# A decode step with gated attention: gate weights and w_down with w_q's second part exchange buffers, and 128 columns of w_o come by a DMA of their own

## The chip, the cores and the metric

The kernel runs on one core of one Trainium2 chip. Its time is the device time of one execution in microseconds (us), the median of some runs. All data is fp32. The engines named here: PE (TensorE, matrix products), DVE (VectorE), ACT (ScalarE), POOL (GpSimd), and SP (SyncE), which computes nothing and issues nearly all transfers. SBUF is the memory on the core with 128 partitions; PSUM takes what PE computes; HBM is the main memory.

## The reference

One decode step, for a batch of 2 and a width of 448. The input is normalised, goes through attention with 16 query heads over 8 cached key/value heads of length 4096, and is gated by a small bilinear network:

```python
xn = layernorm(x)                                   # x: (2, 1, 448)
q = (xn @ wq)                                       # 16 heads of 256
p = softmax(q k^T * 256 ** -0.5)                    # k_cache, v_cache: (2, 8, 4096, 256)
s = (p v) @ wo                                      # wo: (4096, 448)
h = (xn @ w_gate) * (xn @ w_up)                     # 448 -> 1792
g = silu(h @ w_down)
return x + s * g
```

The two caches alone hold 134 MB, the weights 24 MB more. Every byte of them is used once.

## The kernel before

**Recording.** The kernel doesn't call the engines itself. `Recorder` (L206) notes each operation with what it reads and writes; `settle` (L88) derives from it which operation must wait for which; `issue` of `Flow` (L144) then writes each engine's instructions in the recorded order. So each engine runs its own list in order, and an instruction that waits holds back all behind it on that engine. Since every operation passes through the recorder, nearly all rows of the profile have the one line L220; they are told apart by tile names. `loop` (L112) turns PE's part of the seven equal turns into a loop; the other engines' lists are written out.

**Memory.** Two ring buffers of 64 KB a partition (`ring`, L242) and one slot of 52.5 KB a partition (`slot`, L243) take all large loads. Eight PSUM banks, two pairs (`s`) and four alone (`o`, `cb`, `sm`, `wide`), take the products.

**Loads.** `plan` (L275) notes the loads, `issue(n)` (L263) records the next n of them on SP, so the order in which SP issues them is the order of the plan:

- w_q's first part (`wq0`) into ring buffer 1, its first 7,168 columns
- gate and up weights (`wg wu`, the tensor wgu) into the slot
- w_down and w_q's second part (`wd wq1`, the tensor wdq) into ring buffer 0
- the keys of the first item (`k0`, the tensor named first) into ring buffer 1, behind `wq0`
- then for i = 0 to 13 the values of item i with the keys of item i + 1 (`vk`), 8 MB each, into ring buffers 0, 1, 0, 1 and so on; after the second of them w_o's first 24 blocks of 448 columns (`wo`), into the slot
- at the end keys and values of the last items, and the last 8 blocks of w_o (`wo2`), in seven pieces (the tensors last0 and last1)

`issue(4)` (L291) records the first four at the very start; none of them waits. The first turn records two vk loads and then w_o's; each later turn records two. A load that goes into a buffer waits on SP until the last reader of what lies there is done.

**Compute.** An item is one key/value head of one batch row; there are 16. Before the loop, the normalisation runs on DVE and POOL, PE computes the query's first half (`query(0)`, reading `wq0`), the gate (`ffn_in`, reading `wg` and `wu`; `ffn_out`, reading `wd`), the query's second half (`query(1)`, reading `wq1`), and the first scores (`scores(0)`, reading `k0`), in this order (L517 to L523). Each of the seven turns (L524) does two items. For item i: softmax of its scores (DVE, PE, ACT), the product with the values on PE (`values`), a copy of the result on DVE, a copy of the next item's query into one of two small tiles (`qc`, L537, on ACT), and the next item's scores on PE, which read that copy. At a turn's end the two items are combined and divided by their sums. After the loop come the last two items, interleaved with the product with w_o (`project`, L506, over 24 blocks; `project_last`, L512, over the last 8), and the gate; one store of 56 KB ends the kernel.

**Host side.** Inputs are laid out for the loads before the launch (L584 to L622): each load is one array of 128 rows, and a row goes to one partition.

Of the kernel before, what the change touches and what calls it, by code (L numbers as in the profile page):

```python
# [8 lines left out]
B, D = 2, 448  # L9
# [11 lines left out]
LATE = 24  # L21
PART = 14 * (D + 512)
EPS = 1e-5
WQ = 14 * 512
LEAD = 0


class Flow:
# [115 lines left out]
    def issue(self):  # L144
        nc = self.nc
        lead = nc.alloc_semaphore("lead")
        for _ in range(LEAD):
            nc.vector.sem_inc(lead)
# [72 lines left out]
        return add  # L221


def gated_decode_block(nc, x, first, vk, last0, last1, wq0, wdq, wo, wgu, out):
    flow = Flow(nc)
    PE, DVE, ACT, POOL, SP = [getattr(flow, e) for e in ("PE", "DVE", "ACT", "POOL", "SP")]
    names = iter(range(1000))
# [14 lines left out]
    ring = Ring("ring", [128, 2 * ROW], 2, 512)  # L242
    slot = Ring("slot", [128, PART], 1, 512)  # L243
# [7 lines left out]
    def two():  # L251
        pairs.append(pairs.pop(0))
        return pairs[-1]

    def bank(name=None):
        return banks[name] if name else two()[:, 0]
# [6 lines left out]
    def issue(n=1):  # L263
        for names, place, src, cuts in todo[:n]:
            t = place()
            width = ROW if not names[0].startswith("w") else src.shape[1] // len(names)
            for i, name in enumerate(names):
                loaded[name] = t[:, i * width:(i + 1) * width]
            if names == ["wd", "wq1"]:
                loaded["wd"], loaded["wq1"] = t[:, :14 * D], t[:, 14 * D:]  # L270
            for lo, hi in zip(cuts, cuts[1:]):
                SP.dma_start(t[:, lo:hi], src[:, lo:hi])
        del todo[:n]

    def plan(names, place, src, cuts=None):  # L275
        todo.append((names.split(), place, src, cuts or [0, src.shape[1]]))
# [2 lines left out]
        return ring.bufs[1][:, WQ:]  # L279

    plan("wq0", lambda: ring.bufs[1], wq0)
    plan("wg wu", slot, wgu)
    plan("wd wq1", lambda: ring.bufs[0], wdq)
    plan("k0", behind, first)
    for i in range(LAST):
        plan(f"v{i} k{i + 1}", ring, vk[i])
# [2 lines left out]
    plan(f"k{LAST + 1} v{LAST}", ring, last0, [0, ROW, 2 * ROW])  # L289
    plan(f"v{LAST + 1} wo2", ring, last1, [0, 6144, ROW, *(ROW + i * D for i in (5, 7, 8))])  # L290
    issue(4)  # L291


# [131 lines left out]
    def query_of(i):  # L425
        g, b = divmod(i, B)
        return qT[g // 4][:, b, g % 4].rearrange("p d r j -> p d (r j)")

    def scores(i, q, s, halves=(0, 1)):
        k = loaded[f"k{i}"].rearrange("p (h d c n) -> p h d c n", h=2, d=2, c=NT)  # L430
        for h in halves:
            for d in range(2):
                for c in range(NT):
                    PE.matmul(s[W * c:W * (c + 1), h, :], q[:, d], k[:, h, d, c, :], start=d == 0, stop=d == 1)
        return s
# [31 lines left out]
    def softmax(i, s):  # L467
        m = peak(s)
        return turned(exponential(i, s, m, peak_of_all(m)), work["pT"]())
# [4 lines left out]
    def total(add):  # L474
        sm = bank("sm")
        PE.matmul(sm[:, :B], add.rearrange("p a r j -> p (a r j)"), su, start=True, stop=True)
        DVE.reciprocal(over, sm[:, :B])

    def values(i, pT, o):

        for e in range(KB):
            h, t, at = e // 8, e % NT, e % 8 * 2 * W
            PE.matmul(o[W * t:W * (t + 1), :], pT[:, h, at:at + 2 * W:2],
                             loaded[f"v{i}"][:, e * 512:(e + 1) * 512], start=e < NT, stop=e >= KB - NT)

    def combine(ob):
        cb = bank("cb")
        src = ob.rearrange("p s (e d c k) -> p s e d c k", e=2, d=2, c=NT)
        for e in range(2):
            for c in range(NT):  # L490
                PE.matmul(cb[W * c:W * (c + 1), :B * 64], add_blocks[:, e].rearrange("p r j -> p (r j)"),
                                 src[:, :, e, :, c, :], start=e == 0, stop=e == 1)
        return cb[:, :B * 64]

    def turn(oT, g, cb):
        DVE.transpose(oT[:, g].rearrange("p d r (b j) -> p b d r j", b=B),
                      cb.rearrange("p (b d r j) -> p b d r j", b=B, d=2, r=REP))
# [26 lines left out]
    for first in range(0, LAST, B):  # L524
        flow.turn = first
        issue(2)
        if first == 0:
            flow.turn = None
            issue()
            flow.turn = first  # L530
        for i in range(first, first + B):
            p = softmax(i, s)
            o = bank("o")
            values(i, p, o)
            DVE.tensor_copy(ob[:, i % B], o)
            q = copy()
            ACT.copy(q, query_of(i + 1))  # L537
            s = scores(i + 1, q, two())
        total(add_head)
        cb = combine(ob)  # L540
        t = work["h"]()[:, :B * 64]
        DVE.tensor_tensor(t.rearrange("p (s k) -> p s k", s=B), cb.rearrange("p (s k) -> p s k", s=B),
                          over[:, :, None].to_broadcast([128, B, 64]), op=OP.mult)
        turn(oT, first // B, t)
# [19 lines left out]
    t = work["h"]()  # L564
# [62 lines left out]
```

## Time and profile before

| | |
|---|---|
| time, median of 3 runs | 378.86 us (378.81 to 379.39) |
| the profiled execution: its own time | 379.15 us |
| its span, first to last instruction | 377.8 us |
| PE / DVE / ACT / POOL busy, share of the span | 50% / 20% / 8% / 1% |
| data read from HBM | 158.54 MB, 420 GB/s over the span |

A transfer passes over up to 16 DMA engines at once. A packet in the rows of transfers is one piece that one of them moves. "DMA share" in the rows of a stretch is the mean share of the 16 engines' time that the packets started in this stretch take, so a short stretch can show over 1. "us to landing" is from SP's issue to the last byte. Matmuls are written as inner x columns, then the output's shape. An entry in square brackets tells how long the engine stood idle ahead of a row and what ended it. The median of three runs and the profiled execution differ by 0.29 us.

### The profile page before, as it was taken

To read this page: it belongs to the slowest core of one execution; us is meant where nothing else is said; L and a number is where in the kernel's file an instruction comes from. 1 tells how busy PE (TensorE), PEld (TensorE's weight loads), DVE (VectorE), ACT (ScalarE), POOL (GpSimd) and SP (SyncE) were. 2 spreads that over 40 slices of the span, in tenths; PEclk is the share of its full clock that TensorE was granted. 3 is DMA by queue.
4 is the path that set the end of the run, shared out by engine and by line. 5 is a ranking of instruction groups with operands and counts; after the bars stand their busy time and mean duration, and the time that the engine had idled before them with its cause. 6 is when DMAs were issued, how large, how long until landed. Compare 5 with 4: busy or idle time off the path is not lost. (4 is left out here: it accounts for less than half of the span.)

```text
span 377.8 us, 3298 instructions
## 1 busy us (share of the span) xinstructions
PE 189.9 (50%) x1474; PEld 57.6 (15%) x1474; DVE 75.5 (20%) x124; ACT 28.6 (8%) x58; POOL 2.4 (1%) x14
## 2 busy tenths in 40 slices
PE   0827391090730373727282719190909092808776
PEld 0201120020210020202020202020202020202223
DVE  2101013003040021312113211312130304030430
ACT  1101011001010001010101010101010101010120
POOL 0100000000000000000000000000000000000000
PEclk9968598577785585959687968776867766776999
DMA  8999979999999999899999999999999999989995
GB/s 340 474 437 410 412 281 430 402 397 437 433 476 444 444 430 423 382 438 444 444 437 444 444 437 444 430 409 395 444 444 444 437 444 444 437 389 406 435 421 233
DMA packets 3898, 158.68 MB, mean 420 GB/s; under 512 B 562, under 2 KB 692, under 8 KB 820
## 3 DMA queue, kind: packets, MB, share of 16 engines
q1 hardware_dynamic: 3888, 158.59, 97.5%
q8 instruction: 4, 0.07, 0.1%
q14 instruction: 2, 0.02, 0.0%
q10 hardware_dynamic: 4, 0.00, 0.0%
HBM read 158.54 MB, written 0.06 MB: 420 GB/s over the span
## 5 line engine op out<-in xcount | busy, mean ns | idle before, releaser
L220 PE MATMUL o<-ring,pT 128*32 128x512 f32 x480 | 82.4, 848 | 118.2 <-PEq L172 118.2
L220 PE MATMUL s<-ring,qc 128*32 128x512 f32 x448 | 50.7, 592 | 0.0
L220 PEld LDWEIGHTS o<-ring,pT 128*32 128x32 f32 x480 | 20.8, 149 | 167.2 <-issue 167.2
L220 DVE COPY ob<-o 128x512 f32<-128x512 f32 x14 | 9.7, 691 | 159.9 <-PE o L220 159.9
L220 ACT ACTIVATE p<-s,m 128x1024 f32<-128x1024 f32 x16 | 17.8, 1114 | 289.7 <-DVE m L220 289.7
L220 DVE TENSOR_REDUCE m<-s 128x1 f32<-128x1024 f32 x16 | 19.3, 1204 | 21.8 <-PE s L220 21.8
L220 DVE STREAM_TRANSPOSE pT<-p 128x1024 f32<-128x1024 f32 x15 | 18.7, 1245 | 19.1 <-ACT p L220 19.1
L220 PEld LDWEIGHTS s<-ring,qc 128*32 128x32 f32 x448 | 15.1, 110 | 33.2 <-issue 33.2
L220 PE MATMUL sm<-ident,m 128*1 128x128 f32 x16 | 4.4, 276 | 25.6 <-PEq L172 23.7
L220 DVE TENSOR_REDUCE mx<-sm 1x128 f32<-1x512 f32 x16 | 10.9, 679 | 8.1 <-PE sm L220 8.1
L220 PE MATMUL s<-slot,xnT 128*32 128x448 f32 x48 | 7.2, 748 | 7.4 <-DMA slot<-wgu 7.4
L220 PE MATMUL s<-ring,hT 128*32 128x448 f32 x28 | 5.5, 903 | 8.4 <-DMA ring<-wdq 8.4
L220 PE MATMUL sm<-one,mx 1*128 1x1 f32 x16 | 3.2, 201 | 12.9 <-PEq L172 12.1
L220 PE MATMUL s<-ring,xnT 128*32 128x512 f32 x48 | 8.1, 825 | 0.0
L220 PE MATMUL s<-ring,qT 128*32 128x512 f32 x64 | 7.5, 597 | 0.0
L220 PEld LDWEIGHTS sm<-ident,m 128*1 128x1 f32 x16 | 1.3, 79 | 35.1 <-issue 32.9
L220 DVE RECIPROCAL over<-sm 128x2 f32<-128x2 f32 x8 | 1.4, 171 | 23.9 <-PE sm L220 23.9
L220 PE MATMUL s<-ident,pT 2*128 2x2 f32 x4 | 0.6, 246 | 10.7 <-DVE pT L220 10.7
L220 PE MATMUL cb<-ob,add_blocks 128*32 128x128 f32 x128 | 5.2, 279 | 0.6 <-ACT ob L220 0.6
L220 PE MATMUL wide<-slot,oT 128*32 128x448 f32 x48 | 4.9, 539 | 0.0
L220 PEld LDWEIGHTS sm<-one,mx 1*128 1x128 f32 x16 | 2.3, 142 | 16.6 <-issue 15.7
L220 PE MATMUL s<-ring,slot 128*32 128x512 f32 x32 | 3.6, 596 | 1.1 <-DMA ring<-last 1.1
(65 smaller groups left out, 63.7 us busy)
## 6 DMA issues: line engine op xcount, KB each, us to landing
ring<-last SPq DMA_DIRECT2D x2, 4096.0 KB, 27.1
ring<-wdq SPq DMA_DIRECT2D x1, 6720.0 KB, 42.4
slot<-wgu SPq DMA_DIRECT2D x1, 6272.0 KB, 25.4
slot<-wo SPq DMA_DIRECT2D x1, 5376.0 KB, 51.1
ring<-first SPq DMA_DIRECT2D x1, 4096.0 KB, 51.4
ring<-wq SPq DMA_DIRECT2D x1, 3584.0 KB, 11.0
ring<-last SPq DMA_DIRECT2D x1, 3072.0 KB, 21.9
ring<-last SPq DMA_DIRECT2D x1, 1120.0 KB, 24.4
```

What stands on the lines that cost most here:

```text
L220: self.flow.record(self.engine, lambda: method(out, *args, **kw), writes, reads, name == "dma_start")
```

## The change

Four things change.

1. The loads of gate and up weights and of w_down with w_q's second part exchange their places: the former goes into ring buffer 0, the latter into the slot. The order of the loads stays.
2. w_o's first load is 128 columns narrower. These 128 columns come by a second DMA right behind it into the same place; its source is an array of 4 groups of 33 rows of 128 columns, of which 32 rows each are read (the 33rd row is filler and isn't read).
3. The copy of the next item's query runs on POOL, not on ACT.
4. `LEAD` is 48: DVE's list begins with 48 instructions that each add one to a semaphore that nobody waits for.

```diff
-LEAD = 0
+LEAD = 48
+SHARE = 4
+COLS = 128
...
-def gated_decode_block(nc, x, first, vk, last0, last1, wq0, wdq, wo, wgu, out):
+def gated_decode_block(nc, x, first, vk, last0, last1, wq0, wdq, wo, wox, wgu, out):
...
             width = ROW if not names[0].startswith("w") else src.shape[1] // len(names)
+            if names == ["wo"]:
+                width = LATE * D
...
             for lo, hi in zip(cuts, cuts[1:]):
                 SP.dma_start(t[:, lo:hi], src[:, lo:hi])
+            if names == ["wo"]:
+                SP.dma_start(t[:, cuts[-1]:LATE * D], wox[:, :128 // SHARE])
...
-    plan("wg wu", slot, wgu)
-    plan("wd wq1", lambda: ring.bufs[0], wdq)
+    plan("wg wu", lambda: ring.bufs[0], wgu)
+    plan("wd wq1", slot, wdq)
...
             q = copy()
-            ACT.copy(q, query_of(i + 1))
+            POOL.tensor_copy(q, query_of(i + 1))
...
-    wo, last[1] = c(wo[:, :LATE * D]), np.concatenate([last[1], wo[:, LATE * D:]], 1)
+    last[1] = np.concatenate([last[1], wo[:, LATE * D:]], 1)
+    wox = np.zeros((SHARE, 128 // SHARE + 1, COLS), np.float32)
+    wox[:, :-1] = wo[:, LATE * D - COLS:LATE * D].reshape(SHARE, 128 // SHARE, COLS)
+    wo = c(wo[:, :LATE * D - COLS])
```

More of the change, by code (lines that the diff above doesn't have):

```diff
@@ L619 @@
     nc = bacc.Bacc("TRN2", target_bir_lowering=False, num_devices=1, dynamic_dma_scratch_size=1024)
-    arrays = dict(x=x, first=first, vk=vk, last0=last[0], last1=last[1], wq0=wq0, wdq=wdq, wo=wo, wgu=wgu)
+    arrays = dict(x=x, first=first, vk=vk, last0=last[0], last1=last[1], wq0=wq0, wdq=wdq, wo=wo, wox=wox, wgu=wgu)
     args = [nc.dram_tensor(n, a.shape, mybir.dt.from_np(a.dtype), kind="ExternalInput").ap()
```

## The prediction

> **What bounds the kernel now.** I read the page first: span, slices, chain.
>
> ```profile
> span 377.8 us, 3298 instructions
> ...
> DMA  8999979999999999899999999999999999989995
> GB/s 340 474 437 410 412 281 430 402 397 437 433 476 444 444 430 423 382 438 444 444 437 444 444 437 444 430 409 395 444 444 444 437 444 444 437 389 406 435 421 233
> ...
> q8 instruction: 4, 0.07, 0.1%
> ...
> q10 hardware_dynamic: 4, 0.00, 0.0%
> HBM read 158.54 MB, written 0.06 MB: 420 GB/s over the span
> ...
> DMA 6%; PE 3%; ACT 0%; DVE 0%; issue 0%
> ```
>
> The DMA engines are at nine tenths nearly everywhere, and the bytes are fixed. Apart from the first and last slices, one slice falls clearly out of the row: the sixth (47 to 57 us), 281 GB/s. The chain shows only the end, because a transfer that merely queues isn't followed further back. So I next asked for stretches around the sixth slice (the columns that count here are the last two, DMA share and GB/s), and for a long stretch behind it.
>
> ```profile
> 1.70:51.50 49.80, 24.28 (x136) 6.20 (x140) 6.52 (x19) 4.51 (x9) 1.58 (x6) 0.79 1.00 425
> 51.50:53.50 2.00, 2.00 (x22) 0.61 (x16) 0.00 (x0) 0.94 (x1) 0.00 (x0) 1.00 0.04 16
> 53.50:55.30 1.80, 1.80 (x16) 0.39 (x18) 0.82 (x2) 0.00 (x0) 0.00 (x0) 1.00 0.00 0
> 115.00:340.00 225.00, 110.27 (x816) 33.55 (x816) 47.27 (x70) 14.72 (x33) 0.00 (x0) 0.73 1.00 432
> ```
>
> From 51.5 to 55.3 us the transfers stand still: 3.8 us. In the first 2 us 16 GB/s x 2.0 us = 32 KB still start, one row of k0 (4096 KB over 128 rows is 32 KB): fifteen engines are dry, one is behind. Elsewhere the rate is 432 GB/s at a share of 1.00. Who is late? SyncE's issues, then PE's work, tell it.
>
> ```profile
> 2.11 0.59 SPq L220 DMA_DIRECT2D ring<-first  x1
> 54.44 3.92 SPq L220 DMA_DIRECT2D ring<-vk  x2
> 58.40 0.44 SPq L220 DMA_DIRECT2D slot<-wo  x1
> 85.01 227.88 SPq L220 DMA_DIRECT2D ring<-vk  x12
> ```
> ```profile
> 34.74 0.97 PE L220 MATMUL s<-slot,oT 128*64 128x448 f32 x4
> 44.08 5.52 PE L220 MATMUL s<-ring,hT 128*32 128x448 f32 x28 [8.36 <-DMA ring<-wdq]
> 53.32 1.08 PE L220 MATMUL s<-ring,oT 128*64 128x512 f32 x4
> 54.33 3.64 PE L220 MATMUL s<-ring,qT 128*32 128x512 f32 x32
> ```
> ```profile
> ring<-first SPq DMA_DIRECT2D x1, 4096.0 KB, 51.4
> ring<-vk SPq DMA_DIRECT2D x1, 21.8
> ring<-vk SPq DMA_DIRECT2D x14, 29.3
> ```
>
> After k0 (the tile named first) SyncE has nothing it may issue until 54.44. The first vk transfer goes into ring buffer 0, where w_down and w_q's second part lie; their last reader is query(1), whose last matmuls start at 53.32 and end at 54.40. k0 has landed at 2.11 + 51.4 = 53.5, so the queue runs out first. This is the only place: the fourteen vk transfers take a median of 29.3 us from issue to landing, while 8,389 KB at 432 GB/s need 19.4; each waits some 10 us behind its predecessor.
>
> **The exchange of buffers.** Ring buffer 0 now holds the gate weights. Their last reader is the end of ffn_in, 34.74 + 0.97 = 35.7 us. SyncE's queue is in order and has only the four first issues ahead, so vk0 can be issued at 35.7, some 16 us before the queue would run dry. The order and sizes of the first four loads are the same, so wdq still releases PE at 44.08 and PE's work up to 58 us stays. vk1 needs ring buffer 1, free after scores(0) at 54.33 + 3.64 = 58.0 as before; by then vk0 is moving from 51.5 to about 71. w_o's load needs the slot free of query(1), 54.4, and is issued behind vk1 as before. vk2 was issued at 85.01 and is not needed before w_o's end near 109. No stall is late next: the whole stream behind k0 moves ahead, and releases move with landings, which keeps the 10 us.
>
> What it saves: 3.8 us of standing still, and a restart. The stretch to 51.5, the other start from empty, shows 425 against 432 GB/s: 49.8 x 7/432 = 0.8 us. For the restart I take that 0.8; bounds: 0.3 (a smaller dip), and 1.5, since vk0 landed at 54.44 + 21.8 = 76.2, 20.9 us after 55.3 instead of 19.4. **Minus 4.6 us** (minus 4.1 to 5.3).
>
> Against it: the hole also let the engine that lagged catch up. It ended k0 up to 2.0 us behind the others (53.5 against 51.5) and started vk0 with them. Without the hole its lag stays to the end. Why it lagged:
>
> ```profile
> q8 instruction: 1, 0.02, 6.0%
> ```
>
> That is the window from 82.5 to 83.5 us: an instruction fetch of 16 KB took 6.0% of 16 engine-microseconds, 0.96 us, on one engine. The page counts four of them, and the same is seen between 42.02 and 43.02 us, just ahead of the laggard. Do such lags reach the end now? Budget: start 1.7, 158.5 MB at 432 GB/s 366.9, hole 4.6: 373.2. The last piece lands at about 375.05 (below), so some 1.9 us are left, about one engine's lag. The end already pays one; a fifth laggard on another engine adds only what it lags more: 2.0 - 1.9, say **plus 0.1** (0 to 0.4). On the same engine as a later fetch it would add its whole lag (first rival).
>
> The Trainium skill, "Runtime: NRT & Kernel Launch", section "Instruction fetch mechanics", says that instructions are refilled in 16 KB blocks through a DMA queue of the sequencer's own, the cost "mostly hidden". The block agrees with the four packets (0.07 MB). Hidden holds for the waiting sequencer; where DMA is the bound, 0.96 us on one engine isn't hidden. By the rule the term would be 0 and the sum 0.1 lower.
>
> **The 128 columns.** w_o's load shrinks by 512 of 43,008 bytes a row, and 128 rows of 512 bytes come by a second DMA, whose source is led by 4. On how many engines does it run? Rows for one and for sixteen:
>
> ```profile
> p<-x ACTq DMA_DIRECT2D x2, 1.8 KB
> ```
> ```profile
> DMA packets 144, 0.06 MB, mean 96 GB/s; under 512 B 144, under 2 KB 144, under 8 KB 144
> ...
> q1 hardware_dynamic: 144, 0.06, 34.4%
> ```
>
> The two one-row loads of x made the four packets of q10: one of data and one of completion each, so one engine. The output's store (376.9 to 377.5 us) made 144: 128 rows and 16 completions. A source led by 4 lies between; I take four engines with 32 rows each. A row of 448 bytes cost at most 34.4% x 0.6 us x 16 / 128 = 0.026 us; the upper neighbour:
>
> ```profile
> ring<-last SPq DMA_DIRECT2D x1, 448.0 KB, 25.2
> ring<-last SPq DMA_DIRECT2D x1, 224.0 KB, 25.2
> ```
> ```profile
> 346.49 3.80 SPq L220 DMA_DIRECT2D ring<-last  x5
> ```
>
> These five issues end at 350.29; with 0.44 us for one (w_o's row) the last begins at 349.85 and lands at 375.05. The one ahead of it has equal latency, so its 224 KB (8 rows of 1,792 bytes an engine) took about 0.5 us, 0.06 a row. So four engines get 32 x 0.026 to 0.06 = 0.8 to 2.0 us; I take 0.8, nearer in size. What is left out, 8 x 512 bytes an engine at 27 GB/s (432/16), is 0.15 us off every engine. Where none of the four lags already, the end gains **0.15**; where one does, it loses 0.7 (to 1.85). Spread over all sixteen it is 8 rows, plus 0.05 to 0.35; on one engine, see the rivals. SyncE's extra issue, about 0.44 us like w_o's, lies in its wait from 58.8 to 85.
>
> The Trainium skill, "DMA: Bandwidth & Descriptors", "Rules for kernel authors", warns that a leading dimension below 16 confines a DMA to that many engines. It speaks against this edit, and makes four engines a rule rather than my choice. Here it costs nothing if those four have room; by the rule alone, without room, the sum would be 0.85 higher.
>
> **The copy of q, and 48 increments.**
>
> ```profile
> L220 ACT COPY qc<-qT 128x64 f32<-128x64 f32 x14 | 3.3, 233 | 0.0
> L220 POOL COPY add_blocks<-rows 128x64 f32<-128x64 f32 x1 | 0.2, 234 | 0.0
> L220 PE MATMUL s<-ring,qc 128*32 128x512 f32 x448 | 50.7, 592 | 0.0
> 7.26 0.61 DVE L220 TENSOR_REDUCE st<-p 2x1 f32<-2x448 f32 x1 [7.26 <-DMA p<-x]
> 9.11 0.07 DVE L220 DVE_READ_ACCUMULATOR pT<-p 2x1 f32 x1
> 26.59 4.71 PE L220 MATMUL s<-slot,xnT 128*32 128x448 f32 x24 [7.36 <-DMA slot<-wgu]
> ```
>
> Fourteen copies go from ACT to POOL: 0.233 against 0.234 us for the same shape. POOL has nothing else after 13 us; its copy waits for scores two steps back to leave the buffer, and only PE waits for it. The matmuls that read it have no idle time ahead of them (0.0), and values run before them. Cost 0; uncovered, 14 x 0.23 = 3.3 us of PE, itself behind transfers. The increments run on DVE ahead of its first work, which waits for x until 7.26 us. At most 0.07 us each (the smallest DVE row, an upper end) is 3.4 us; without x as cover that would still lie under PE's 7.36 us wait. Cost 0. They also make DVE's code 48 instructions longer, and the copies make ACT's 14 shorter, which can move a fetch in time; whose fetch is whose isn't shown. A fetch loads one engine by up to 0.96 us whenever it comes. Effect 0, bounds minus 0.96 and plus 0.96 (off or onto the worst laggard).
>
> **The tail** follows the last transfers.
>
> ```profile
> 346.49 21.88 DMA ring<-last
> ...
> 373.51 2.09 PE s L220 x64
> ```
>
> From 346.49 the chain is the queue; the last matmuls end at 373.51 + 2.09 = 375.6, half a microsecond behind the last landing, then two DVE operations and the store. All of this hangs on landings and shifts with them.
>
> **Sum.** -4.6 + 0.1 - 0.15 = -4.65; with the small bounds that point up I round to **-4.5 us**. The profiled execution took 379.15 (span 377.8), so 374.65; the median of the three runs is 0.29 lower, 378.86, so 374.4. I forecast 374.4, with 373.4 to 375.2 as this case's own range.
>
> **Rivals.** *Lags add up* (0.22): the laggard of 42 us, or one of the four engines with the 512-byte rows, is also one that a later fetch hits. Price 0.7 (rows) to 1.9 (fetch): 375.1 to 376.3, 375.6 in the middle. For it: up to five laggards and four loaded engines among sixteen. Against: the 1.9 us of the budget say that so far the fetches didn't meet.
>
> *The hole only moves* (0.06): a later vk isn't issued in time, since landing and release are now closer; half is given back, 376.7. Against it stands the 10 us of queueing in every step.
>
> *It doesn't do what it says* (0.03): vk0 is still held behind something read after 50 us, and the time stays at 378.9. The order of issues and the readers of the gate weights speak against it.
>
> *Slower* (0.03): the 512-byte DMA runs on a single engine, 128 rows at 0.06 us, 7.7 us. Less 0.15 and the 1.9 us of room to the worst laggard, that is plus 5.65 against -4.6, near 380. It decides from (4.6 + 1.9 + 0.15)/128 = 0.052 us a row; at 0.026 it would still be faster. The source led by 4 speaks against it.
>
> The forecast itself has 0.63, and 0.03 goes to more than 373.4 (a dearer restart and a fetch less). A difference of 0.2% (0.76 us) is what this kernel's measurement can tell from none. Faster: 0.63 + 0.03 + 0.22 + 0.06 = 0.94; same 0.03; slower 0.03. A range of 373.4 to 376.4 holds the forecast and the first rival.
>
> **What would show it.** Right: vk's first issue near 36 us, no stretch without transfers between 51 and 56, vk0 landed near 71.5, last issues and the store some 4.5 us earlier, q's copies under POOL with PE's idle ahead of the scores still 0. Lags adding: the last landings as early as forecast by rate, but the end 1 to 2 us behind. Wrong: a first vk issue still past 50 us, or a new slice below 380 GB/s in the middle.

## The result, and the profile after

The changed kernel took 374.33 us against 378.84: a ratio of 0.988 (95% interval 0.9865 to 0.990). Run once more beside the experiments it took 374.23, 374.49 and 374.57 us, again 0.988 (0.9865 to 0.990) of before (378.59 there). Forecast were 374.4 us and a gain of 4.5. Some executions took over 400 us, with slower transfers from some 100 us on; they are left out everywhere, which leaves a single one of the kernel "all but the exchange" below.

The page of the changed kernel, in its second run: span, slices, bytes.

```profile
span 372.8 us, 3347 instructions
...
DMA  8999999998999999999999999999999999999995
GB/s 345 448 441 404 422 439 450 443 445 390 438 452 436 443 450 429 429 415 436 436 443 450 429 429 401 450 436 443 450 429 436 401 443 436 443 404 439 425 416 231
...
HBM read 158.54 MB, written 0.06 MB: 425 GB/s over the span
```

The sixth slice, 281 GB/s before, is 439 now, and no other slice has dropped in its place. SyncE's issues and the latencies to landing (the first of the two vk rows is the first vk load alone, the second the median of all fourteen):

```profile
2.12 0.71 SPq L222 DMA_DIRECT2D ring<-first  x1
35.25 22.33 SPq L222 DMA_DIRECT2D ring<-vk  x2
57.62 0.43 SPq L222 DMA_DIRECT2D slot<-wo  x1
58.10 0.69 SPq L222 DMA_DIRECT2D slot<-wox  x1
82.41 225.59 SPq L222 DMA_DIRECT2D ring<-vk  x12
...
371.24 0.35 SPq L222 DMA_DIRECT2D res<-gate  x1
```
```profile
ring<-vk SPq DMA_DIRECT2D x1, 37.6
ring<-vk SPq DMA_DIRECT2D x14, 29.4
ring<-last SPq DMA_DIRECT2D x1, 224.0 KB, 25.2
```

The first vk load is issued at 35.25 us instead of 54.44, the output's store at 371.24 instead of 376.23. The stretch that stood empty, and the long stretch behind it (last columns: DMA share, GB/s):

```profile
51.50:55.30 3.80, 3.73 (x34) 0.82 (x30) 0.90 (x2) 0.02 (x1) 0.00 (x0) 1.00 0.90 388
...
115.00:340.00 225.00, 116.27 (x832) 34.96 (x836) 47.28 (x70) 13.26 (x22) 2.38 (x10) 0.71 1.00 433
```

388 GB/s where there were 16 and 0; the rate behind it is the same, 433 after 432. So the time came from this one place, which the experiments bear out.

### The profile page after: what moved, and what is told of

Its sections match the earlier page's. It is cut to its first block, busy times and chain, and to the rows that moved or that the text cites. A ratio compares the mean times of both kernels' runs of the same rounds, so it can differ in the third digit from the quotient of the medians.

```text
span 413.0 us, 3347 instructions
## 1 busy us (share of the span) xinstructions
PE 192.8 (47%) x1474; PEld 58.0 (14%) x1474; DVE 75.5 (18%) x124; ACT 26.8 (6%) x44; POOL 5.6 (1%) x28
## 5 line engine op out<-in xcount | busy, mean ns | idle before, releaser
L222 PE MATMUL o<-ring,pT 128*32 128x512 f32 x480 | 86.0, 882 | 146.6 <-PEq L174 146.6
L222 PE MATMUL s<-ring,xnT 128*32 128x448 f32 (+1 forms) x72 | 10.8, 750 | 8.9 <-DMA ring<-wgu 8.9
L222 PE MATMUL sm<-one,mx 1*128 1x1 f32 x16 | 3.3, 209 | 12.8 <-PEq L174 12.1
L222 PE MATMUL s<-ring,qT 128*32 128x512 f32 x64 | 8.9, 693 | 0.0
L222 PE MATMUL s<-slot,hT 128*32 128x448 f32 x28 | 4.7, 769 | 8.9 <-DMA slot<-wdq 8.9
L222 POOL COPY qc<-qT 128x64 f32<-128x64 f32 x14 | 3.3, 238 | 322.3 <-PE s L222 315.6
L222 PE MATMUL s<-ring,oT 128*32 128x112 f32 (+2 forms) x76 | 5.0, 314 | 0.4 <-DMA ring<-last 0.4
L222 PEld LDWEIGHTS s<-ring,xnT 128*32 128x32 f32 x72 | 2.6, 143 | 17.5 <-DMA ring<-wgu 9.8
## 6 DMA issues: line engine op xcount, KB each, us to landing
ring<-first SPq DMA_DIRECT2D x1, 4096.0 KB, 51.4
```

Of the source, the lines that this page charges most:

```text
L222: self.flow.record(self.engine, lambda: method(out, *args, **kw), writes, reads, name == "dma_start")
```

## The experiments

All times are medians; the kernel before, run beside each of three sets of experiments, took 378.59, 378.76 and 378.51 us, so a difference of 0.2 us between kernels of different sets says little. "Exchange alone" is the kernel before with the two `plan` lines of the diff and nothing else. The changed kernel itself came first, for its profile:

> The changed kernel, unaltered, for a profile that can be compared with the one of before. Theory (the hole closes): 374.3 us, 0.988 of before; vk's first issue near 35.3 us, no stretch without transfers between 51 and 56 us, vk0 landed at 71 to 73, the last piece of w_o landed near 370.6 instead of 375.05, the store issued near 371.7. Rival (lags add up): the last landings of most engines 4.6 us earlier, but one engine over 2 us behind the others at the end.

374.49 us, as told above: no stretch without transfers, the first vk load issued at 35.25 and landed at 35.25 + 37.6 = 72.85.

**The exchange, and all the rest, each by itself.**

```diff
-    plan("wg wu", slot, wgu)
-    plan("wd wq1", lambda: ring.bufs[0], wdq)
+    plan("wg wu", lambda: ring.bufs[0], wgu)
+    plan("wd wq1", slot, wdq)
```

> The kernel before with the exchange of buffers alone (q's copy on ACT, no increments, w_o's first load in one piece). Theory (the hole is nearly all of it): 374.3 to 374.6 us, 4.3 to 4.6 below before. Rival (the other three edits carry a part by relieving engines that lag): 375 to 376, and then the other edits by themselves gain about 1 us.

Measured: 374.10 us (374.02 to 374.14), 0.987 of before (0.986 to 0.989). The exchange alone gives 4.5 us, the whole gain, and a little more than the changed kernel has.

The changed kernel with those two lines put back:

> The changed kernel with the two loads back in their old buffers: 128 columns by themselves, q's copy on POOL, 48 increments. Theory: within 0.4 us of before, 378.4 to 378.9, and the stretch from 51.5 to 55.3 us empty again. Rival (the other edits carry a part): 377.5 to 378.

That single execution took 378.48 us; the kernel before has 378.2 to 379.5. The profile is of another, longer execution, but these two stretches lie ahead of its slow part and show the hole where it was:

```profile
51.50:53.50 2.00, 2.00 (x22) 0.62 (x16) 0.00 (x0) 0.94 (x1) 0.00 (x0) 1.00 0.04 16
53.50:55.30 1.80, 1.80 (x16) 0.39 (x18) 0.81 (x2) 0.00 (x0) 0.00 (x0) 1.00 0.00 0
```

**Is it the moment of release?** With the buffers exchanged, one small PE product that reads the gate weights is added at three places. The first vk load must wait for it; the result is used by nobody.

```diff
     ffn_out()
     query(1)
     s = scores(0, query_of(0), two())
+    PE.matmul(banks["cb"][:W, :W], xnT[:, 0, :], loaded["wg"][:, :W], start=True, stop=True)
```

> The exchange of buffers alone, and one added PE product (128x32 by 128x32, result unused) behind the first scores that reads the gate weights, so that the first vk load waits for it, until 58.1 us instead of 36. This doubles the suspected wait: the queue runs dry at 51.5 and starts again some 0.9 us after the issue. Theory (every microsecond of standing still is a microsecond of time, plus the restart): the hole is 59.0 - 51.5 = 7.5 us, plus 0.8, less up to 0.4 for the laggard that catches up: 374.1 + 8.0 = 382.1 us. Rival (part of a stall is made up later, the stream has slack): under 380.5.

382.0 us (381.78 to 382.85), 1.009 of before (1.006 to 1.012): dearer than before by the longer stall, as forecast. The same line one step earlier, behind `query(1)`:

> The exchange of buffers alone, with one added small PE product behind query(1) that reads the gate weights: the first vk load waits for the same moment as in the kernel before, about 54.6 us, though the buffers are exchanged. Theory (the moment of release is all there is to the exchange): 378.4 to 378.8, the kernel before. Rival (the place of the data has an effect of its own): 374 to 377.

379.22 us (377.95 to 380.04), 1.0015 of before (1.0003 to 1.0027): the gain is gone although the buffers are exchanged. It lies 0.4 above the range I gave, and what adds that isn't shown. And behind `ffn_out()`:

> The exchange of buffers alone, with the same added product behind ffn_out: the first vk load is issued near 50.8 us instead of 36, about 0.9 us before its first byte moves, so as the queue runs dry (51.3 to 51.8). Theory (only standing still costs): 374.1 to 374.6. Rival (a load must be queued well ahead to start without a loss): 375 or more.

375.28 us (374.63 to 375.99). Put side by side, with the first vk issue and the time of the same, profiled execution:

| release behind | first vk issue, us | time, us |
|---|---|---|
| ffn_in (exchange alone) | 36.09 | 374.14 |
| ffn_out | 49.63 | 374.63 |
| query(1), buffers exchanged | 53.41 | 377.95 |
| query(1), kernel before | 54.44 | 379.15 |
| the first scores | 57.29 | 381.78 |

From 53.41 to 57.29 the issue moves by 3.88 us and the time by 3.83: a microsecond for a microsecond. The restart can be read off as well. The first fifteen rows of 64 KB behind the hole, in the kernel before, and fifteen such rows in the middle of the first vk load of the exchange alone:

```profile
55.30:55.95 0.65, 0.65 (x12) 0.17 (x8) 0.08 (x1) 0.00 (x0) 0.00 (x0) 1.00 4.48 1512
```
```profile
53.45:54.40 0.95, 0.95 (x8) 0.20 (x4) 0.00 (x0) 0.00 (x0) 0.00 (x0) 1.00 2.39 1035
```

Rate times stretch is 983 KB in both, fifteen rows. Share times stretch times 16 engines, divided by fifteen, gives 3.1 us a row behind the hole and 2.4 us without one: the first rows take 0.7 us longer after standing still.

At 49.63 the queue isn't dry yet, so there is no hole, and still the profiled execution is 0.5 us longer than the exchange alone, and the median 1.2 us. By its number the run falls to the rival; the rival's mechanism isn't shown. The first rows, fifteen of 64 KB and one of 32 KB, hold a share of 2.89:

```profile
51.10:51.95 0.85, 0.85 (x12) 0.11 (x4) 0.00 (x0) 0.05 (x1) 0.00 (x0) 1.00 2.89 1195
```

That is some 2.5 us for a row of 64 KB, only 0.1 longer than without a pause, and the first vk load lands at 49.63 + 23.3 = 72.9 against 36.09 + 36.6 = 72.7 with the exchange alone and 72.85 in the changed kernel. So at most 0.2 us come from the late issue; where the rest of the 0.5 comes from stays open. The three executions of 375.2 to 376.0 have no profile; whether PE simply came later there, so that the queue did run dry, stays open too.

**The three small edits.** First the changed kernel without the 128 columns (`plan` and the host code of w_o as before):

> The changed kernel with w_o's first load in one piece again, nothing else altered. Theory: 0.15 us slower than the changed kernel (the 512 bytes a row that all engines were spared, 374.4 to 374.6), with the last landing's slowest engine later by the same. Rival (one of the four engines with the small rows is a laggard): 0.7 us faster than the changed kernel, 373.6.

374.82 us, but in two groups: 374.44 and 374.50, as the theory has it, and 375.14 and 375.18. The profiled execution is one of the second group; its chain of waits runs through PE in the tail, as in the kernels below. Then the exchange with each edit alone:

```diff
-            ACT.copy(q, query_of(i + 1))
+            POOL.tensor_copy(q, query_of(i + 1))
```

> The exchange of buffers and q's copy on POOL, nothing else. The exchange alone took 374.1 us, all four edits 374.2 to 374.6, all without the 128 columns 374.4 to 375.2. Theory (none of the three small edits has a price of its own; the transfers set the end): 374.1, within 0.2. Rival (the copy on POOL lets PE start scores at other moments, and PE's clock is then granted otherwise in the tail): 374.4 to 375.2 with values spread over two groups 0.7 us apart, as without the 128 columns.

374.87 us (374.65 to 375.09): 0.77 above the exchange alone.

```diff
-LEAD = 0
+LEAD = 48
```

> The exchange of buffers and the 48 increments on DVE, nothing else. Theory: 374.1, within 0.2; the 8 KB fetch seen at 158 us after the exchange alone comes near 13 us, and loads one engine as before. Rival (the moved fetch meets an engine that lags anyway, or the later start of DVE costs): 374.4 to 375.2.

374.59 us: 0.5 above it, with four executions at 374.25 to 374.70 and two at 375.09 and 375.19. The fetch came at 12.8 us instead of 158.4, and the last piece landed at 369.8, no later than with the exchange alone (370.1), so the transfers don't carry the 0.5.

The third is the exchange with the change's lines for `wox`, `SHARE` and `COLS`, and neither POOL's copy nor increments:

> The exchange of buffers and the 128 columns by themselves, nothing else (q's copy on ACT, no increments). Theory (12 engines are spared 0.15 us, four take 0.7 more and have the room): 373.95, 0.15 below the exchange alone. Rival (one of the four is among those that lag): 374.8, 0.7 above it.

373.99 us (373.85 to 374.07), against 374.02 to 374.14 for the exchange alone: 0.1, less than the kernel before moved between the two sets. How many engines carry the small rows can be read off the changed kernel between 102 and 105 us, in 40 slices:

```profile
GB/s 0 0 0 0 0 1748 0 874 2622 1502 642 1809 942 61 61 75 61 68 61 2628 20 27 20 20 20 20 27 20 20 888 0 0 874 0 874 0 0 0 0 1748
```

Between rows of 64 KB (the large numbers) there are 61 to 75 GB/s, later 20 to 27: at first three engines, then one alone, at about 21 GB/s. A row of 512 bytes at 21 GB/s takes 0.024 us. From 103.46 to 104.3 us, where the one is alone, it has

```profile
DMA packets 35, 0.08 MB, mean 98 GB/s; under 512 B 2, under 2 KB 34, under 8 KB 34
```

so 34 - 2 = 32 rows of 512 bytes, a quarter of the 128. Four engines with 32 rows each carry it, and one of them comes some 0.8 us after the others: a laggard is among them, though the end isn't set by it.

**Where do 0.8 us come from that no transfer explains?** The chain of waits of the exchange with POOL's copy, in order of time (start, duration, what), and for contrast that of the exchange alone:

```profile
336.74 6.50 PE o L220 x32
343.24 3.43 PE s L220 x32
...
349.87 3.31 PE s L220 x16
...
355.18 3.01 PE wide L220 x32
...
359.38 3.57 PE o L220 x32
362.95 1.50 PE wide L220 x16
...
364.77 3.62 PE s L220 x32
...
369.79 1.58 PE s L220 x64
```
```profile
336.65 5.03 PE o L220 x32
341.68 1.77 PE s L220 x15
...
343.78 25.78 DMA ring<-last
```

With POOL's copy the tail hangs on PE from 336.7 us to the end; otherwise it ends on a transfer. Both start at 336.7 us with the same 32 products, in 6.50 and in 5.03 us. Stretches of the two, first with POOL's copy (the granted clock is the third number from the end):

```profile
336.70:342.50 5.80, 5.76 (x28) 1.58 (x32) 0.00 (x0) 0.00 (x0) 0.00 (x0) 0.50 1.03 446
349.00:353.00 4.00, 3.50 (x17) 0.67 (x17) 1.12 (x2) 0.00 (x0) 0.00 (x0) 0.57 1.10 471
```
```profile
336.70:342.50 5.80, 5.80 (x44) 1.77 (x48) 0.69 (x1) 0.00 (x0) 0.00 (x0) 0.76 1.05 452
349.00:353.00 4.00, 4.00 (x41) 1.20 (x37) 1.48 (x3) 1.21 (x2) 0.00 (x0) 1.00 1.10 471
```

Nearly the same DMA, but PE's clock is 0.50 and 0.57 instead of 0.76 and 1.00. The Trainium skill, "TensorE: Matmul & The Clock Gate", Part 1, says that PE is at half rate by default and gets the full one after a busy window of about 3.4 us; the window runs freely, so the moment depends on where the work falls in it. The trace agrees as to the two levels, and the same products, started within 0.1 us of each other, get a different clock; what sets the moment isn't shown here.

The landings tell who is the bound. The last piece lands at 345.8 + 24.2 = 370.0 us with POOL's copy, and at 344.3 + 25.8 = 370.1 with the exchange alone, so the transfers don't end later. The output's store is, first with POOL's copy:

```profile
372.00 0.35 SPq L220 DMA_DIRECT2D res<-gate  x1
```
```profile
371.22 0.35 SPq L220 DMA_DIRECT2D res<-gate  x1
```

As a second test, 16 of the 24 blocks of w_o's product at the end are left out:

```diff
         for i in range(lo, hi):
+            if NT <= i < LATE - NT:
+                continue
             t = i % NT
```

> The exchange of buffers with q's copy on POOL (374.65 to 375.09 us), and 16 of the 24 blocks of w_o in the product at the end left out (heads 4 to 19 of 32 halves; the output is without them). PE has 32 matmuls of 0.54 us a lane less, some 3.2 us, between the last items. Theory (with a low clock between 328.7 and 342.5 and again near 349 us PE itself becomes the bound of the tail): 374.1, as the exchange alone, the chain of waits ends on the last pieces' landing again. Rival (transfers end later with the copy on POOL): unchanged, 374.7 to 375.1.

374.12 us (373.91 to 374.46), and the chain ends on a transfer again:

```profile
343.54 24.74 DMA ring<-last
...
368.32 2.04 PE s L220 x64
```

The rival falls: with the copy on POOL the transfers can end as early as before. But this run doesn't tell less work from a better clock. Its profiled execution has, ahead of the blocks left out, the clock of the exchange alone:

```profile
336.70:342.50 5.80, 5.80 (x41) 1.61 (x45) 0.62 (x1) 0.00 (x0) 0.00 (x0) 0.73 1.03 446
```

That PE set the end with POOL's copy rests on the chain and on the landings. The same blocks left out in the changed kernel:

> The changed kernel with the same 16 blocks of w_o's product left out. Theory (its executions of 374.4 to 374.6 are partly held by PE in the tail): 374.0 to 374.2 in every run, a narrower spread. Rival (transfers alone set the end of the changed kernel): unchanged, 374.2 to 374.6.

374.35 us (374.25 to 374.48): unchanged, the rival holds. The changed kernel isn't held by PE, and yet it is 0.3 slower than the exchange alone, with the same span, 372.8 us. The difference lies outside the span. Time less span, over all executions:

| kernels | time less span, us |
|---|---|
| with the 48 increments (five kernels) | 1.60 to 1.73 |
| without them (the kernel before and seven others) | 1.26 to 1.46 |

The two groups don't touch. The 48 increments cost some 0.33 us ahead of the first or behind the last instruction that the profile spans; what does it there isn't shown.

**A version that beats both** came out of this: the exchange with the 128 columns, 373.99 us (0.987 of before, 0.985 to 0.990), and the exchange alone, 374.10. Against the changed kernel's 374.2 to 374.6 that is 0.3 to 0.5 us.

## Why the prediction was right, point by point

- **The hole, minus 4.6.** Right in place and mechanism. The first vk issue was forecast for 35.7 and came at 35.25; the exchange alone gained 4.49; the runs with a later release show a slope of one. The restart, 0.8 in my sum: a hole of 57.29 + 0.96 (issue to first byte, 54.44 to 55.4 in the kernel before) - 51.5 = 6.75 us cost 381.78 - 374.14 = 7.64, which leaves 0.9 for it; the same reckoning leaves 0.9 for the release behind query(1) and 1.1 for the kernel before. The first rows themselves show 0.7.
- **The laggard, plus 0.1.** Its lag isn't lost any more: k0 still lands at 2.12 + 51.4 = 53.5, and the first vk load 19.35 us later, at 72.85, which is one full transfer. My marker "landed near 71.5" forgot this, though the sum had it. The last piece lands at 344.88 + 25.2 = 370.1, forecast 375.05 - 4.65 = 370.4. Whether a lag adds the 0.1 at the end is too small to be told.
- **The 128 columns, minus 0.15.** About minus 0.1 in the run by itself, at the edge of what can be told; in the changed kernel the last piece lands no earlier with the columns than without them (370.1 and 369.9). So the term isn't shown. The four engines and the row price (0.026 forecast, 0.024 read off) were right. One of the loaded engines does lag, as in the first rival, but not so much that it sets the end.
- **The copy and the increments, "Cost 0".** This step was wrong. The copies run on POOL, at 0.238 us each, and the scores have no idle time ahead of them, as forecast:

```profile
L222 PE MATMUL s<-ring,qc 128*32 128x512 f32 x448 | 50.7, 592 | 0.0
...
L222 POOL COPY qc<-qT 128x64 f32<-128x64 f32 x14 | 3.3, 238 | 291.8 <-PE s L222 285.3 <-DVE qT L222 6.5
```

  But with the exchange alone, the copy cost 0.77 and the increments 0.5 us. Of the latter, 0.33 lie outside the span, where my argument, which looked only for cover inside it, couldn't see them. In the profiled executions of both, the rest is PE in the tail: the chain of waits runs through PE, though the last piece lands at 370.0 and 369.8, no later than the 370.1 of the exchange alone.
- **The tail, "all of this hangs on landings and shifts with them".** Wrong as a rule: PE was close behind the transfers, and in some executions a stretch at half clock puts it ahead. By their times these are all six with POOL's copy alone, two of six with the increments alone and two of four without the 128 columns; one of each has a profile. This rival, PE becoming the bound of the tail, was missing from my list; its price is 0.6 to 0.8 us. In the changed kernel, whose profiled chain ends on a transfer, it doesn't decide. Whether the copy or the increments shift the clock's stretches, and whether the 128 columns shift them back, isn't settled; the execution with POOL's copy and the blocks left out had the better clock although its instructions were the same up to there.
- **The sum.** Forecast was minus 4.5; measured were minus 4.5 at first (378.84 to 374.33) and minus 4.1 beside the experiments (378.59 to 374.49). The measured parts, exchange minus 4.5, columns about minus 0.1, increments plus 0.33, add up to minus 4.3, between the two. The copy's 0.77 doesn't appear in the whole, and why it doesn't is open. My rounding from 4.65 to 4.5 covered errors of about the size of the missed terms; that was luck in part.

## What to carry to other kernels

In a kernel bound by transfers, look for the stretch in which none runs, and ask which buffer's last reader holds back the next issue; put into that buffer what is read earliest. An issue that comes after the queue has run dry costs a microsecond for a microsecond and some 0.7 to 1.1 us for the restart; how far ahead it has to come isn't settled here. What lies outside the span and what PE's clock does in the tail can be worth more than small rebalancing edits, so try such edits one at a time on top of the main one.

## What the runs showed that was not expected

The old release at query(1) made the time depend on PE's clock near 45 us. PE's last products ahead of it, in the kernel before and in the one held behind query(1):

```profile
44.08 5.52 PE L220 MATMUL s<-ring,hT 128*32 128x448 f32 x28 [8.36 <-DMA ring<-wdq]
```
```profile
43.72 4.67 PE L220 MATMUL s<-slot,hT 128*32 128x448 f32 x28 [8.91 <-DMA slot<-wdq]
```

The same 28 products took 5.52 or 4.67 us, and the release came at 54.44 or 53.41. It fits that kernels held by this release spread over more (before: 377.7 to 380.2; held behind query(1): 377.95 to 380.04) than the exchange alone (374.02 to 374.14). There the same products can be slow without harm, in the execution of 374.14 us:

```profile
43.96 5.86 PE L220 MATMUL s<-slot,hT 128*32 128x448 f32 x28 [7.91 <-DMA slot<-wdq]
```

In the changed kernel they took 4.63 us and the execution 374.49. So an early release takes the time off PE's clock, as far as these four profiled executions show it. And 48 semaphore increments that nobody waits for, hidden inside the span, cost 0.33 us outside it.
